# Split q and k in buffers per head, at two points of a pair's steps, and squares by ScalarE's Square

## The chip, the cores and the metric

One core of a Trainium2 chip runs the kernel. The metric is device time in microseconds (us) of one execution. The engines are named as in the profile: PE is TensorE (PEld its weight loads), DVE is VectorE, ACT is ScalarE, POOL is GpSimd, SP is the queue that issues all of this kernel's DMAs.

## The reference

Windowed attention with sink tokens feeds a two-layer network without a gate. `x` is the attention's output with the heads side by side, 3072 tokens by 512.

```python
# q, k, v: 4 batches x 8 heads x 768 positions x 64, float32; n_sink 4, window 128
scores = (1 / sqrt(64)) * q @ k.T
keep = (pos_k < n_sink) | ((pos_q - pos_k >= 0) & (pos_q - pos_k < window))
a = exp(where(keep, scores, -1e9) - max);  a = a / (sum(a) + 1e-9)
x = (a @ v)                                # w_in 512 x 2048, w_out 2048 x 512, float64
h = maximum(x @ w_in, 0);  out = (h * h) @ w_out
```

## The kernel before

The work is cut into 8 chunks of 384 tokens (`TOK`), half a sequence each, named `c`. The eight heads of a chunk go in four pairs, named `p`; `hh` is the head in the pair and `i` (0 to 2) the block of 128 queries. A tile's name in the program carries these numbers: `s_6_3_1_2` is the score of chunk 6, pair 3, head 1, block 2.

For precision a float32 number is carried as a rounded high part and the rest, both in the reduced format float32r. From pair 8 on (chunk 2) the scores are taken from such split tiles: `KS` holds high and low part of k, and `QS` the high part of q in 64 partitions and its low part in the other 64. `prep_q` makes `QS` with two casts on ACT (L215) and two subtractions on DVE (L217); `prep_k` makes `KS` with a cast on DVE (L223) and a subtraction on POOL (L224). There is one buffer of each (`ap1`), and one of the raw `qn` and `kn`.

A pair's steps are: six scores (L254 on PE; DVE's L258 adds the mask and takes the minimum into `nbs`; ACT's L261 takes the Exp and the sum), with a `normalise` on POOL behind the third and the sixth (L278, L283, and the sink columns into `PSK`, L289 and L292; DVE gives the reciprocal of the sums, L271 and L272). Then, while the next pair's scores run: transposes of head 0 and head 1 (`probs_of`, tile `pt`, copied out by DVE into `PTF`, L358 to L363), of the sinks' columns (`sink_keys`, tile `pss`), and the products with v (`values`, tile `xo`, L382). The scores, `pt` and `pss` share two PSUM banks in turn (tag `att`).

The network of an earlier chunk fills PE between these steps. For each of 16 slices of 128 hidden units there are 12 matmuls into `ph` (L454, weights `wi` in two parts against `x` in two parts), ACT's Relu into `r` (L462), the product `ph * r` on DVE (L466), its high part `gh` by a cast on ACT (L467), its low part `gl` on DVE (L471), and 9 matmuls into `po` for the slice before (L484, per token block two with `gh` and one with `gl`).

`slot(s)` lists the steps of pair `s`, mixed with the last steps of pair `s - 1`; the main loop deals these units out between the network's. Up to chunk 1 the order on each engine is that of the code (`manual_schedule`); from the first pair of chunk 2 on (`PAUSE`) a scheduler orders each engine's queue by the order of the code as priority and by its own costs. Every queue runs in order. `check_row` puts two more instructions on ACT now and then (L577, L579).

Of the kernel before, what the change touches and what calls it, by code (L numbers as in the profile page):

```python
# [40 lines left out]
def sink_window_attention_moe(  # L41
# [25 lines left out]
    with ExitStack() as fast:  # L67
# [143 lines left out]
        def prep_q(c, p):  # L211
            st = state[c, p]
            st["QS"] = QS = ap1.tile([P, 2, TOK], F32R, tag="QS", name=f"QS_{c}_{p}")
            for hh, own, oth in HALVES:
                nc.scalar.copy(QS[own, hh, :], st["qn"][own])  # L215
            for hh, own, oth in HALVES:
                nc.vector.tensor_tensor(QS[oth, hh, :], st["qn"][own], f32(QS[own, hh, :]), op=ALU.subtract)  # L217

        def prep_k(c, p):
            st = state[c, p]  # L220
            nk = st["nk"]
# [1 line left out]
            nc.vector.tensor_copy(KS[:, :, 0, 0:nk], st["kn"][:, :, 0:nk])  # L223
            nc.gpsimd.tensor_tensor(KS[:, :, 1, 0:nk], st["kn"][:, :, 0:nk], f32(KS[:, :, 0, 0:nk]), op=ALU.subtract)  # L224
# [5 lines left out]
        def score(c, p, hh, i, tag="att"):  # L230
# [16 lines left out]
            if c * NPAIR + p < NPS:  # L247
                own = HALVES[hh][1]
                KF = st["kn"][:, hh].rearrange("p n c -> p (n c)")
                nc.tensor.matmul(ps[:, 0:n], st["qn"][own, qcols], KF[own, c0 : c0 + n], start=True, stop=True)  # L250
            else:
                flat = st["KS"][:, hh].rearrange("p a n c -> p a (n c)")
                for a in range(2):
                    nc.tensor.matmul(  # L254
                        ps[:, 0:n], st["QS"][:, hh, qcols], flat[:, a, c0 : c0 + n], start=(a == 0), stop=(a == 1)
                    )
# [157 lines left out]

        def slot(s):

            nop = lambda: None
# [2 lines left out]
            pr = [nop] * 3  # L420
            if s + 1 < len(pairs) and s + 1 != PAUSE:
                n = pairs[s + 1]
                split = s + 1 >= NPS
                pr = [
                    lambda: split and prep_q(*n), lambda: split and prep_k(*n),
                    lambda: s + 2 != PAUSE and start_pair(s + 2),
                ]
            if s == PAUSE:
                units = sc + pr
            else:  # L430
                va = values_of(pairs[s - 1])
# [10 lines left out]
        def moe(legs):  # L442
# [3 lines left out]
            for n in range(len(items) + 1):  # L446
                if n < len(items):
# [18 lines left out]
                    nc.vector.tensor_tensor(ph[:, 0:TOK], ph[:, 0:TOK], r, op=ALU.mult)  # L466
                    nc.scalar.copy(gh, ph[:, 0:TOK])  # L467
# [484 lines left out]
```

## Time and profile before

| | |
|---|---|
| median of 3 runs | 737.74 us (737.46 to 737.82) |
| the profiled execution | 738.48 us, span of its instructions 736.6 us |
| busy share of the span | PE 95%, PEld 81%, DVE 68%, ACT 52%, POOL 30% |
| granted TensorE clock, mean | 0.991 |

A stretch in which PE is idle is lost to the whole, since PE's matmuls fill nearly all of the span; the other engines matter where PE waits for one of them. Matmuls overlap in the records, so a busy PE may still run below its pace.

### The profile page before, as it was taken

The page shows a single profiled execution, that of the slowest core. Times are in us where ns is not written, and L with a number is a line of the kernel's source. Part 1 is how long each engine was busy: PE and PEld are TensorE (multiplying, and loading weights), DVE is VectorE, ACT ScalarE, POOL GpSimd, SP SyncE. Part 2 cuts the span into 40 slices and gives each one's busy share as a digit, 9 for nine tenths or more (in the row PEclk, how much of TensorE's full clock was granted, in tenths as well). Part 3 has the DMA queues.
Part 4 walks back from the last instruction along what each step waited for, and adds up shares of the span by engine and source line. Part 5 has one row for each costly group of instructions (what it writes and reads, how often), then busy time and mean ns, then how long its engine had stood idle before and what let it go on. Part 6 is the DMA issues. An engine that isn't in the chain of part 4 may idle for free.

```text
span 736.6 us, 11643 instructions
## 1 busy us (share of the span) xinstructions
PE 698.4 (95%) x3866; PEld 599.6 (81%) x3866; DVE 502.4 (68%) x1254; ACT 381.2 (52%) x1074; POOL 223.6 (30%) x408
## 2 busy tenths in 40 slices
...
GB/s 233 154 177 186 130 140 191 176 91 60 133 60 81 156 91 70 97 129 91 100 99 77 133 112 88 96 114 113 95 60 112 85 55 16 1 1 44 0 1 47
DMA packets 37010, 71.75 MB, mean 97 GB/s; under 512 B 4368, under 2 KB 14096, under 8 KB 36944
## 3 DMA queue, kind: packets, MB, share of 16 engines
...
q8 instruction: 32, 0.52, 0.3%
...
## 4 chain that ended last, share of the span: by engine, by line
PE 63%; DVE 11%; ACT 3%; issue 3%; POOL 1%; DVEq 0%; POOLq 0%; ACTq 0%
PE po L484 26%; PE ph L454 25%; PE xo L382 4%; PE s L254 4%; DVE QS L217 3%; DVE rs L271 2%; PE pt L352 2%; DVE ph L466 1%; PE xo L385 1%; PE pss L299 1%; ACT P L261 1%; DVE gl L471 1%; ACT gh L467 1%; DVE KS L223 1%; DVE PTF L358 1%
## 5 line engine op out<-in xcount | busy, mean ns | idle before, releaser
L454 PE MATMUL ph<-x,wi 128*128 128x384 f32 x1536 | 309.9, 341 | 0.0
L454 PEld LDWEIGHTS ph<-x,wi 128*128 128x128 f32 x1536 | 265.4, 188 | 8.3 <-issue 1.7
L484 PE MATMUL po<-wo,gh 128*128 128x512 f32 x768 | 244.8, 399 | 4.9 <-ACT gh L467 4.9
L484 PEld LDWEIGHTS po<-wo,gh 128*128 128x128 f32 x768 | 136.7, 189 | 25.7 <-ACT gh L467 7.8
L484 PE MATMUL po<-wo,gl 128*128 128x512 f32 x384 | 152.8, 398 | 0.0
L261 ACT ACTIVATE P<-P,nbs 128x264 f32<-128x264 f32 (+1 forms) x192 | 94.7, 494 | 106.7 <-DVE nbs L258 95.6
L466 DVE TENSOR_TENSOR ph<-ph,r 128x384 f32<-128x384 f32 x128 | 71.9, 562 | 77.3 <-ACT r L462 76.7
L278 POOL TENSOR_TENSOR P<-P 128x256 f32<-128x256 f32 (+1 forms) x48 | 44.2, 921 | 246.8 <-ACT P L261 246.8
L467 ACT CAST gh<-ph 128x384 fp32r<-128x384 f32 x128 | 60.9, 476 | 98.6 <-DVE ph L466 97.5
L462 ACT ACTIVATE r<-ph 128x384 f32<-128x384 f32 x128 | 62.0, 484 | 90.2 <-PE ph L454 89.0
L283 POOL TENSOR_SCALAR P<-P,rs 128x136 f32<-128x136 f32 (+2 forms) x192 | 85.1, 460 | 61.7 <-DVE rs L272 30.3
L471 DVE TENSOR_TENSOR gl<-ph,gh 128x384 fp32r<-128x384 f32 x128 | 70.9, 554 | 42.6 <-ACT gh L467 41.6
L224 POOL TENSOR_TENSOR KS<-kn,KS 128x816 fp32r<-128x816 f32 (+1 forms) x24 | 59.2, 2465 | 102.2 <-DVE KS L223 67.2
L484 PEld LDWEIGHTS po<-wo,gl 128*128 128x128 f32 x384 | 72.2, 188 | 19.5 <-DVE gl L471 3.8
L258 DVE CUSTOM_DVE_ANT_0 P<-s,maskA 128x264 f32<-128x264 f32 x128 | 53.4, 426 | 40.2 <-PE s L254 38.4
L254 PE MATMUL s<-KS,QS 128*128 128x264 f32 (+1 forms) x288 | 58.7, 283 | 5.7 <-POOL KS L224 4.4
L254 PEld LDWEIGHTS s<-KS,QS 128*128 128x128 f32 x288 | 52.1, 188 | 13.8 <-POOL KS L224 5.4
L271 DVE TENSOR_SCALAR rs<-sm 128x3 f32<-128x3 f32 (+1 forms) x56 | 54.1, 967 | 8.3 <-ACT P L261 7.3
L382 PE MATMUL xo<-PTF,vn 128*64 128x256 f32 x448 | 48.3, 354 | 0.8 <-ACT PTF L341 0.7
L217 DVE TENSOR_TENSOR QS<-qn,QS 64x384 fp32r<-64x384 f32 x48 | 46.4, 966 | 2.2 <-ACT QS L215 0.8
L382 PEld LDWEIGHTS xo<-PTF,vn 128*64 128x64 f32 x448 | 32.3, 141 | 17.2 <-issue 6.3
L358 DVE TENSOR_TENSOR PTF<-pt,halves 128x256 f32<-128x256 f32 x96 | 36.2, 414 | 6.3 <-PE pt L352 6.0
...
## 6 DMA issues: line engine op xcount, KB each, us to landing
...
kn<-in_k_dram SPq DMA_DIRECT2D x24, 272.0 KB, 4.3
...
```

The lines of the kernel that those rows point to most:

```text
L217: nc.vector.tensor_tensor(QS[oth, hh, :], st["qn"][own], f32(QS[own, hh, :]), op=ALU.subtract)
L254: nc.tensor.matmul(ps[:, 0:n], st["QS"][:, hh, qcols], flat[:, a, c0 : c0 + n], start=(a == 0), stop=(a == 1))
L261: nc.scalar.activation(Pt[:, i, 0:n], Pt[:, i, 0:n], AF.Exp, bias=nb, scale=-1.0, accum_out=sm[:, i : i + 1])
L271: nc.vector.tensor_scalar(rs[:, hs], st["sm"][:, hs], EPS, None, op0=ALU.add)
L283: nc.gpsimd.tensor_scalar(Pt[:, j, 0:n], Pt[:, j, 0:n], rs[:, hh, j : j + 1], 1.0, op0=ALU.mult, op1=ALU.mult)
L382: nc.tensor.matmul(xo[h * D : h * D + D, cols], lhsT, rhs, start=(n == 0), stop=False, skip_group_check=True)
L454: nc.tensor.matmul(ph[:, 0:TOK], wi_at(i, cc, fc), xt[:, cc, :], start=(m == 0), stop=(m == 3 * NCC - 1),)
L462: nc.scalar.activation(r, ph[:, 0:TOK], AF.Relu)
L466: nc.vector.tensor_tensor(ph[:, 0:TOK], ph[:, 0:TOK], r, op=ALU.mult)
L467: nc.scalar.copy(gh, ph[:, 0:TOK])
L471: late = lambda: nc.vector.tensor_tensor(gl, ph[:, 0:TOK], f32(gh), op=ALU.subtract)
L484: nc.tensor.matmul(po[t], gt[:, ts_], wo[f][:, i, :], start=(f == f0 and j == 0), stop=(f == f1 - 1 and j == 2),)
```

## The change

`prep_q` and `prep_k` become `prep(s, hh)`, which makes one head's `KS` and `QS` in buffers of that head's own. In a pair's steps, `prep` of the next pair's head 0 stands behind the third score, that of head 1 behind the sixth, and the load of the next raw q and k (and this pair's v) opens the pair's steps. The transposes of head 1 now come ahead of the sinks'. In the network, `gh` is no longer a cast of the product but ACT's Square of `r`, issued right behind Relu; the product, for `gl`, stays on DVE.

```diff
-        def prep_q(c, p):
-            st["QS"] = QS = ap1.tile([P, 2, TOK], F32R, tag="QS", name=f"QS_{c}_{p}")
-            for hh, own, oth in HALVES:
-                nc.scalar.copy(QS[own, hh, :], st["qn"][own])
-            for hh, own, oth in HALVES:
-                nc.vector.tensor_tensor(QS[oth, hh, :], st["qn"][own], f32(QS[own, hh, :]), op=ALU.subtract)
-        def prep_k(c, p):
-            st["KS"] = KS = ap1.tile([P, 2, 2, 4, BS], F32R, tag="KS", name=f"KS_{c}_{p}")
-            nc.vector.tensor_copy(KS[:, :, 0, 0:nk], st["kn"][:, :, 0:nk])
-            nc.gpsimd.tensor_tensor(KS[:, :, 1, 0:nk], st["kn"][:, :, 0:nk], f32(KS[:, :, 0, 0:nk]), op=ALU.subtract)
+        def prep(s, hh):
+            _, own, oth = HALVES[hh]
+            KS = ap1.tile([P, 2, 4, BS], F32R, tag=f"KS{hh}", name=f"KS_{c}_{p}_{hh}")
+            QS = ap1.tile([P, TOK], F32R, tag=f"QS{hh}", name=f"QS_{c}_{p}_{hh}")
+            nc.vector.tensor_copy(KS[:, 0, 0:nk], st["kn"][:, hh, 0:nk])
+            nc.gpsimd.tensor_tensor(KS[:, 1, 0:nk], st["kn"][:, hh, 0:nk], f32(KS[:, 0, 0:nk]), op=ALU.subtract)
+            nc.scalar.copy(QS[own, :], st["qn"][own])
+            nc.vector.tensor_tensor(QS[oth, :], st["qn"][own], f32(QS[own, :]), op=ALU.subtract)
...
-                lambda: probs_of(*a, 0), lambda: sink_keys(*a), lambda: probs_of(*a, 1), lambda: values(*a),
+                lambda: probs_of(*a, 0), lambda: probs_of(*a, 1), lambda: sink_keys(*a), lambda: values(*a),
...
-                units = [
-                    sc[0], va[0], sc[1], va[1], sc[2], va[2], sc[3], va[3], sc[4], sc[5],
-                    pr[0], pr[1], pr[2],
-                ]
+            units = [
+                lambda: start_pair(s + 1), sc[0], va[0], sc[1], va[1], va[2], sc[2], lambda: prep(s + 1, 0),
+                va[3], sc[3], sc[4], sc[5], lambda: prep(s + 1, 1),
+            ]
...
                     nc.scalar.activation(r, ph[:, 0:TOK], AF.Relu)
-                    yield
                     gh = mp.tile([P, TOK], F32R, tag="gh", name=f"gh_{c}_{fc}")
                     gl = mp.tile([P, TOK], F32R, tag="gl", name=f"gl_{c}_{fc}")
+                    nc.scalar.activation(gh, r, AF.Square)
+                    yield
                     nc.vector.tensor_tensor(ph[:, 0:TOK], ph[:, 0:TOK], r, op=ALU.mult)
-                    nc.scalar.copy(gh, ph[:, 0:TOK])
```

The raw q and k of odd pairs in the first eight, which borrowed the `QS` and `KS` buffers, borrow those of head 0 now.

What this makes of the engines' queues is shown at one place, from the last score of pair (6,3) into pair (7,0). The line numbers of the changed kernel differ: L222 to L225 are `prep` (L223, L224, L215 and L217 before); the attention's are 1 higher (L259 is L258); in the network L441 is L454, L454 is L466, L458 is L471 and L471 is L484.

DVE before, from the mask of the last score on (rows that repeat are left out):

```order
L258 ISA P_6_3_1_6164,nbs_150<-s_6_3_1_2_6222,maskA_100 128x264
L223 CAST KS_7_0_6259<-kn_7_0_6036 128x2x544
L217 TENSOR_TENSOR QS_7_0_6244<-qn_7_0_6035,QS_7_0_6244 64x384
L271 TENSOR_SCALAR rs_6_3_1_6227<-sm_6_3_6049 128x3
L272 RECIPROCAL rs_6_3_1_6227<-rs_6_3_1_6227 128x3
L466 TENSOR_TENSOR ph_5_10_6215<-ph_5_10_6215,r_5_10_6242 128x384
L471 TENSOR_TENSOR gl_5_10_6250<-ph_5_10_6215,gh_5_10_6249 128x384
L258 ISA P_7_0_0_6286,nbs_150<-s_7_0_0_0_6287,maskA_100 128x264
```

DVE after, at the same place:

```order
L454 TENSOR_TENSOR ph_5_10_6290<-ph_5_10_6290,r_5_10_6309 128x384
L458 TENSOR_TENSOR gl_5_10_6312<-ph_5_10_6290,gh_5_10_6311 128x384
L259 ISA P_6_3_1_6297,nbs_150<-s_6_3_1_2_6326,maskA_100 128x264
L222 CAST KS_7_0_1_6349<-kn_7_0_6123 128x544
L225 TENSOR_TENSOR QS_7_0_1_6350<-qn_7_0_6122,QS_7_0_1_6350 64x384
L272 TENSOR_SCALAR rs_6_3_1_6331<-sm_6_3_6147 128x3
L273 RECIPROCAL rs_6_3_1_6331<-rs_6_3_1_6331 128x3
L454 TENSOR_TENSOR ph_5_11_6355<-ph_5_11_6355,r_5_11_6375 128x384
L458 TENSOR_TENSOR gl_5_11_6378<-ph_5_11_6355,gh_5_11_6377 128x384
L259 ISA P_7_0_0_6388,nbs_150<-s_7_0_0_0_6389,maskA_100 128x264
```

Half a cast and one subtraction stand between the last score and the reciprocal, where the whole cast and two subtractions stood, and the product and low part of slice 10 have moved ahead of that score.

POOL before, between the normalising of head 0 and of the next pair's head 0:

```order
L292 TENSOR_TENSOR PSK_142<-P_6_3_0_6050,PSK_142 128x2x8
L224 TENSOR_TENSOR KS_7_0_6259<-kn_7_0_6036,KS_7_0_6259 128x2x544
L278 TENSOR_TENSOR P_6_3_1_6164<-P_6_3_1_6164 128x2x128
L283 TENSOR_SCALAR P_6_3_1_6164<-P_6_3_1_6164,rs_6_3_1_6227 128x128
L283 TENSOR_SCALAR P_6_3_1_6164<-P_6_3_1_6164,rs_6_3_1_6227 128x136 x2
L289 CAST PSK_142<-P_6_3_1_6164 128x4x8
L278 TENSOR_TENSOR P_7_0_0_6286<-P_7_0_0_6286 128x3x128
```

POOL after:

```order
L293 TENSOR_TENSOR PSK_142<-P_6_3_0_6148,PSK_142 128x2x8
L223 TENSOR_TENSOR KS_7_0_1_6349<-kn_7_0_6123,KS_7_0_1_6349 128x544
L279 TENSOR_TENSOR P_6_3_1_6297<-P_6_3_1_6297 128x2x128
L284 TENSOR_SCALAR P_6_3_1_6297<-P_6_3_1_6297,rs_6_3_1_6331 128x128
L284 TENSOR_SCALAR P_6_3_1_6297<-P_6_3_1_6297,rs_6_3_1_6331 128x136 x2
L290 CAST PSK_142<-P_6_3_1_6297 128x4x8
L223 TENSOR_TENSOR KS_7_1_0_6495<-kn_7_1_6363,KS_7_1_0_6495 128x544
L279 TENSOR_TENSOR P_7_0_0_6388<-P_7_0_0_6388 128x3x128
```

A half of k stands ahead of the normalising of each head, where the whole stood ahead of head 1's.

PE before, from head 0's transposes on, in pair (7,0)'s first half (the rows of `ph` stand there twice, those of `po` three times or more):

```order
L352 MATMUL pt_6_3_0_6313<-ident_94,P_6_3_0_6050 128x128 x3
L484 MATMUL po_5_0_2_5722<-wo_10_1523,gh_5_10_6249 128x512 x2
L484 MATMUL po_5_0_2_5722<-wo_10_1523,gl_5_10_6250 128x512
L254 MATMUL s_7_0_0_1_6329<-KS_7_0_6259,QS_7_0_6244 128x264 x2
L454 MATMUL ph_5_12_6334<-x0_5_4741,wi_136 128x384 x2
L454 MATMUL ph_5_12_6334<-x1_5_4742,wi_136 128x384
L299 MATMUL pss_6_3_6341<-ident_94,PSK_142 128x128 x2
L254 MATMUL s_7_0_0_2_6353<-KS_7_0_6259,QS_7_0_6244 128x264 x2
L352 MATMUL pt_6_3_1_6386<-ident_94,P_6_3_1_6164 128x128 x3
```

PE after:

```order
L353 MATMUL pt_6_3_0_6406<-ident_94,P_6_3_0_6148 128x128 x3
L441 MATMUL ph_5_12_6413<-x0_5_4810,wi_136 128x384 x2
L441 MATMUL ph_5_12_6413<-x1_5_4811,wi_136 128x384
L255 MATMUL s_7_0_0_1_6420<-KS_7_0_0_6255,QS_7_0_0_6256 128x264 x2
L353 MATMUL pt_6_3_1_6436<-ident_94,P_6_3_1_6297 128x128 x3
L471 MATMUL po_5_0_0_5777<-wo_11_1565,gh_5_11_6377 128x512 x2
L471 MATMUL po_5_0_0_5777<-wo_11_1565,gl_5_11_6378 128x512
L300 MATMUL pss_6_3_6459<-ident_94,PSK_142 128x128 x2
L255 MATMUL s_7_0_0_2_6470<-KS_7_0_0_6255,QS_7_0_0_6256 128x264 x2
```

Head 1's transposes come 14 matmuls behind head 0's and ahead of the sinks', and the third score comes last.

More of the change, by code (lines that the diff above doesn't have):

```diff
@@ L209, in sink_window_attention_moe @@
         HALVES = ((0, lo_, hi_), (1, hi_, lo_))
-        def prep_q(c, p):
-            st = state[c, p]
-            st["QS"] = QS = ap1.tile([P, 2, TOK], F32R, tag="QS", name=f"QS_{c}_{p}")
-            for hh, own, oth in HALVES:
-                nc.scalar.copy(QS[own, hh, :], st["qn"][own])
-            for hh, own, oth in HALVES:
-                nc.vector.tensor_tensor(QS[oth, hh, :], st["qn"][own], f32(QS[own, hh, :]), op=ALU.subtract)
-        def prep_k(c, p):
+        def prep(s, hh):
+            if s >= len(pairs):
+                return
+            c, p = pairs[s]
             st = state[c, p]
             nk = st["nk"]
-            st["KS"] = KS = ap1.tile([P, 2, 2, 4, BS], F32R, tag="KS", name=f"KS_{c}_{p}")
-            nc.vector.tensor_copy(KS[:, :, 0, 0:nk], st["kn"][:, :, 0:nk])
-            nc.gpsimd.tensor_tensor(KS[:, :, 1, 0:nk], st["kn"][:, :, 0:nk], f32(KS[:, :, 0, 0:nk]), op=ALU.subtract)
+            _, own, oth = HALVES[hh]
+            KS = ap1.tile([P, 2, 4, BS], F32R, tag=f"KS{hh}", name=f"KS_{c}_{p}_{hh}")
+            QS = ap1.tile([P, TOK], F32R, tag=f"QS{hh}", name=f"QS_{c}_{p}_{hh}")
+            st["KS", hh], st["QS", hh] = KS, QS
+            nc.vector.tensor_copy(KS[:, 0, 0:nk], st["kn"][:, hh, 0:nk])
+            nc.gpsimd.tensor_tensor(KS[:, 1, 0:nk], st["kn"][:, hh, 0:nk], f32(KS[:, 0, 0:nk]), op=ALU.subtract)
+            nc.scalar.copy(QS[own, :], st["qn"][own])
+            nc.vector.tensor_tensor(QS[oth, :], st["qn"][own], f32(QS[own, :]), op=ALU.subtract)
         def bank(tag, name):
@@ L251, in score @@
             else:
-                flat = st["KS"][:, hh].rearrange("p a n c -> p a (n c)")
+                flat = st["KS", hh].rearrange("p a n c -> p a (n c)")
                 for a in range(2):
                     nc.tensor.matmul(
-                        ps[:, 0:n], st["QS"][:, hh, qcols], flat[:, a, c0 : c0 + n], start=(a == 0), stop=(a == 1)
+                        ps[:, 0:n], st["QS", hh][:, qcols], flat[:, a, c0 : c0 + n], start=(a == 0), stop=(a == 1)
                     )
```

22 lines of the change are left out of this document (4 added, 18 removed).

## The prediction

> **What bounds the kernel now.** I read the page's busy times and chain first, then the busy times by stage, then who TensorE (PE) waits for, then the timeline around one wait.
>
> ```profile
> PE 698.4 (95%) x3866; PEld 599.6 (81%) x3866; DVE 502.4 (68%) x1254; ACT 381.2 (52%) x1074; POOL 223.6 (30%) x408
> ...
> PE 63%; DVE 11%; ACT 3%; issue 3%; POOL 1%; DVEq 0%; POOLq 0%; ACTq 0%
> ```
>
> PE is busy 95% of the span and holds 63% of the chain that ended last. The change keeps every matmul, so it can only give back time in which PE stands still or runs slow: 736.6 - 698.4 = 38.2 us of idle PE. Where that lies (columns: the stretch, its length, busy time and instructions of PE, weight loads, DVE, ACT and POOL, granted clock, DMA):
>
> ```profile
> 0.00:99.00 99.00, 80.49 (x446) 59.35 (x447) 79.23 (x248) 67.11 (x177) 45.93 (x97) 0.97 0.55 172
> 99.00:153.00 54.00, 54.00 (x286) 48.77 (x285) 50.71 (x117) 33.96 (x69) 4.97 (x9) 1.00 0.53 171
> 153.00:231.50 78.50, 73.47 (x410) 63.33 (x409) 61.90 (x151) 33.57 (x91) 31.15 (x53) 0.98 0.27 76
> 231.50:317.50 86.00, 84.94 (x489) 74.64 (x489) 60.85 (x147) 50.44 (x157) 31.25 (x57) 1.00 0.38 111
> 317.50:406.00 88.50, 84.86 (x472) 72.53 (x471) 58.44 (x142) 49.79 (x157) 29.32 (x52) 1.00 0.35 98
> 406.00:490.50 84.50, 84.50 (x489) 74.48 (x489) 61.11 (x144) 50.33 (x157) 30.39 (x52) 1.00 0.36 106
> 490.50:579.00 88.50, 84.89 (x471) 72.52 (x470) 58.82 (x144) 49.81 (x157) 29.33 (x52) 1.00 0.35 97
> 579.00:665.00 86.00, 85.52 (x490) 75.12 (x489) 51.21 (x129) 30.05 (x78) 21.28 (x38) 1.00 0.09 25
> 665.00:736.60 71.60, 65.69 (x329) 58.86 (x327) 20.11 (x36) 16.11 (x33) 0.00 (x0) 0.98 0.07 24
> ```
>
> The start-up to 99 us holds 99 - 80.5 = 18.5 us of it, the end after 665 us 5.9 us. Scores there use unsplit q and k, or there are none, and only the squares change: I take nothing for both. In between PE idles 0, 5.03, 1.06, 3.64, 0, 3.61 and 0.48 us: 13.8 us. The stretches 317.5 to 406 and 406 to 490.5 each hold four pairs of heads; the second runs without a gap and is 4.0 us shorter. Who PE waits for from 140 us on (us in total, times, longest):
>
> ```profile
> PE po L484 <- ACT gh L467: 4.9, 5, 1.5
> PE s L254 <- POOL KS L224: 4.4, 4, 2.5
> PE pss L299 <- DVE PTF L361: 3.0, 7, 0.6
> PE s L254 <- DVE nbs L258: 1.4, 2, 0.9
> ```
>
> These four rows are 4.9 + 4.4 + 3.0 + 1.4 = 13.7 us, all but 0.1 of the idle time in the middle. Beside them weight loads (PEld) come late without PE going idle at once:
>
> ```profile
> PEld po L484 <- ACT gh L467: 7.8, 9, 1.8
> ...
> PEld po L484 <- DVE gl L471: 3.8, 13, 0.3
> ```
>
> One such place word for word: the end of pair (6,3), where the next pair's q and k are split (start, length, engine and line, in brackets the idle time before and its releaser):
>
> ```profile
> 545.59 0.41 PE L254 MATMUL s<-KS,QS 128*128 128x264 f32 x2
> ...
> 546.03 0.43 DVE L258 CUSTOM_DVE_ANT_0 P<-s,maskA 128x264 f32<-128x264 f32 x1 [1.56 <-PE s L254]
> 546.07 1.03 ACT L215 CAST QS<-qn 64x384 fp32r<-64x384 f32 x2
> ...
> 546.39 0.72 DVE L223 CAST KS<-kn 128x1088 fp32r<-128x1088 f32 x1
> ...
> 547.12 0.52 ACT L261 ACTIVATE P<-P,nbs 128x264 f32<-128x264 f32 x1
> 547.15 0.55 DVE L217 TENSOR_TENSOR QS<-qn,QS 64x384 fp32r<-64x384 f32 x1
> 547.25 2.85 POOL L224 TENSOR_TENSOR KS<-kn,KS 128x1088 fp32r<-128x1088 f32 x1 [7.25 <-DVE KS L223]
> ...
> 547.84 2.28 DVE L271 TENSOR_SCALAR rs<-sm 128x3 f32<-128x3 f32 x1
> ...
> 550.05 0.74 POOL L278 TENSOR_TENSOR P<-P 128x256 f32<-128x256 f32 x1
> 550.15 1.05 DVE L217 TENSOR_TENSOR QS<-qn,QS 64x384 fp32r<-64x384 f32 x1
> ...
> 551.23 0.18 DVE L272 RECIPROCAL rs<-rs 128x3 f32<-128x3 f32 x1
> ...
> 551.33 0.54 DVE L466 TENSOR_TENSOR ph<-ph,r 128x384 f32<-128x384 f32 x1
> 551.51 1.08 POOL L283 TENSOR_SCALAR P<-P,rs 128x128 f32<-128x128 f32 x3 [0.72 <-DVE rs L272]
> ...
> 551.90 0.48 ACT L467 CAST gh<-ph 128x384 fp32r<-128x384 f32 x1 [3.79 <-DVE ph L466]
> ...
> 552.41 0.56 DVE L471 TENSOR_TENSOR gl<-ph,gh 128x384 fp32r<-128x384 f32 x1 [0.55 <-ACT gh L467]
> ...
> 552.43 0.72 PE L484 MATMUL po<-wo,gh 128*128 128x512 f32 x2 [0.84 <-ACT gh L467]
> ```
>
> The last score ends near 546.0. From 547.25 to 550.10 POOL works out the low parts of k (L224). VectorE's (DVE) tiny L271 starts at 547.84 and takes 2.28 us, until POOL is through; the next L217 takes 1.05 us beside L278 instead of the 0.55 us of the one before. The squares (L466) come at 551.33, gh waits 3.79 us for them, and PE stands 0.84 us for gh.
>
> The Trainium skill, page "SBUF — State Buffer", section "Who interferes with whom", says that VectorE and GpSimd lock a shared port for a whole instruction and that the second to issue fully blocks. The rows above agree: 2.28 us for one DVE instruction and 1.05 us for another. By that rule the change also adds 24 lockings; the fourth rival says where that would bite.
>
> **The change part by part.**
>
> Splitting per head. Before, one KS and one QS buffer serve a pair, so the split can begin only behind the pair's sixth score, and the next pair's first score waits for it. Now head 0's halves are made behind the third score, about ten us ahead of their use, head 1's behind the sixth, with three scores, transposes and value matmuls between. The wait for KS (4.4 us) goes. Its longest, 2.5 us near 156 us, was followed by this:
>
> ```profile
> 156.20:160.20 4.00, 4.00 (x13) 3.58 (x14) 4.00 (x11) 2.62 (x6) 0.25 (x1) 0.57 0.62 168
> ```
>
> At a clock of 0.57, 4.0 us lose 4.0 x 0.43 = 1.7 us, and with the gap gone I count that as won too.
>
> The Trainium skill, page "TensorE: Matmul & The Clock Gate", Part 1, has the clock fall only after an idle window of about 3.4 us. PE's gap here was 2.5 us, so the trace differs, and the measurement decides. By that rule the drop would have another cause and could stay; the time would be 721.5 instead of 719.8 us.
>
> What the halves cost:
>
> ```profile
> L224 POOL TENSOR_TENSOR KS<-kn,KS 128x1088 fp32r<-128x1088 f32 x12 | 33.3, 2776 | 50.9 <-DVE KS L223 49.4 <-DVE rs L272 1.6
> ...
> L224 POOL TENSOR_TENSOR KS<-kn,KS 128x816 fp32r<-128x816 f32 x12 | 25.9, 2155 | 51.3 <-PE ph L454 32.1 <-DVE KS L223 17.8 <-DVE rs L272 1.3
> ```
>
> (2776 - 2155) / 272 elements = 2.28 ns per element and 294 ns fixed, so halves of 544 and 408 elements take 1.53 and 1.22 us: 24 x (1.53 + 1.22) = 66 us instead of 59.2, bounds 59 (halves exactly) and 118 (a half as dear as a whole). I take 66, since the two rows give the slope and hold lockings already. POOL is 30% busy. Each half stands ahead of its head's normalising, where the whole one stood ahead of head 1's alone: for head 0 up to 1.5 us, hidden by the half pair until its transposes, for head 1 see below. The k cast on DVE (0.72 us at 546.39) becomes two, together 0.72 to 1.44 us; I take 0.9, near the lower end, as L224's fixed part is small too. Even 0.72 more for each of four pairs adds 2.9 us to the 61.9 of 78.5 us of the densest stage, 153 to 231.5. The two q casts on ACT and two subtractions on DVE stay in number and move apart.
>
> The loads. `start_pair(s + 1)` now opens a pair's units where `start_pair(s + 2)` closed those of the pair before: the same point on SP's queue. New is that the first reader comes half a pair later, not a whole one. A pair takes 84.5 / 4 = 21 us, so about 10 us are left, less about 2 us until the last reader of the old k is through, for this landing:
>
> ```profile
> kn<-in_k_dram SPq DMA_DIRECT2D x24, 272.0 KB, 4.3
> ```
>
> 8 us against 4.3 us: hidden. If not, the split of head 0 slips, which still has some 8 us to its use.
>
> Square of r on ACT. The high part of the squares now follows Relu at once and waits for nothing.
>
> ```profile
> L471 DVE TENSOR_TENSOR gl<-ph,gh 128x384 fp32r<-128x384 f32 x128 | 70.9, 554 | 42.6 <-ACT gh L467 41.6 <-PE pt L352 0.5
> ...
> L467 ACT CAST gh<-ph 128x384 fp32r<-128x384 f32 x128 | 60.9, 476 | 98.6 <-DVE ph L466 97.5
> ...
> L577 ACT ACTIVATE sq<-half 128x256 bf16<-128x256 f32 x64 | 27.5, 429 | 0.5 <-DMA half<-in_moe_w_out_dram 0.4
> ```
>
> The cast at 476 ns is replaced by Square of the same shape; bounds 476 and 429 x 384 / 256 = 644 ns. I take 480, near the cast, the row of equal shape: nothing for ACT, 52% busy; at 644 it is 128 x 0.17 = 22 us on an engine with 355 us idle. DVE's low part gl no longer waits 0.55 us behind its own product for gh: 41.6 us of waiting go from the head of DVE's queue. gl itself still needs the product, so it is what could be late next.
>
> DVE's chain at the place above, reworked: L258 ends 546.47; half a cast 0.4; half L224 1.53, to 548.4, the subtraction of q (0.55) locked in beside it; ACT has one q cast less, so the Exp ends before that; L278 0.74 to 549.15 with L271 beside it; L272 0.18; product 0.54; gl 0.56: 550.4 instead of 552.97, 2.5 us earlier. PE wanted gh at 552.43 - 0.84 = 551.59 and gl two matmuls later, near 551.9. So the 4.9 us for gh go and no wait for gl replaces them. The wait of pss (3.0 us) is for DVE's copies of the transposes, which stand behind a gl that waits 0.55 us for gh, seven times 0.43 us on average; it goes too, as pss now stands behind pt of head 1 and more products. The two waits for nbs (1.4 us) I count as the same lateness of DVE.
>
> New order of transposes. Head 1's now come ahead of the sinks'. From the last score to them PE has 45 matmuls at (6,3); at 84.5 / 489 = 0.173 us each that is 7.8 us. POOL's normalising (L283) ended 552.59, 7.0 us behind the score's start, and by the sum above ends near 550.3, 4.7 us behind it. In 153 to 231.5 us, at pair (2,2), only 30 matmuls stand between, 5.2 us. If DVE is busy there some of three pairs wait: bounds 0 and 3 x (7.0 - 5.2) = 5.4 us; I take 1.0, as the chain there is shortened as well.
>
> The sum by stages: 153 to 231.5, 5.0 + 1.7 = 6.7; 231.5 to 317.5, 1.1; 317.5 to 406 between 3.6 (idle alone) and 88.5 - 472 x 0.173 = 6.9, I take 5.3, since a late load is partly hidden under the matmul ahead; 490.5 to 579 the same, 5.3; 579 to 665, 0.5. Together 18.9, less 1.0: 17.9 us. The profiled execution took 738.48 us (span 736.6 and 1.9 around it), so 720.6; the median of the runs, 737.74, is 0.7 below it: 719.8 us. With every upper bound, 1.7 + 1.7 + 1.0 more and nothing new: 715.4.
>
> **The rivals.**
> Second: the lock lasts as long as before and gl takes gh's place. For: gl hangs on the same DVE queue, and 13 late loads already wait for it. Against: L224's halves. At (6,3) gl would come right behind the product, 551.87 + 0.56 = 552.43, 0.5 us behind its need, so 0.5 / 0.84 of the 4.9 us stay (2.9), the 3.0 us of pss come back at pt, and the late loads (2 x 1.7) stay: 18.9 - 9.3 = 9.6 us won, 738.5 - 9.6 - 0.7 = 728.2 us.
> Third: no change, 736.3 to 739.2, the waits only passed on from pair to pair. Against: 406 to 490.5 shows that the same work runs without any.
> Fourth, slower: the transposes of head 1 wait for POOL in every pair, since half an L224 stands ahead of the normalising and the doubled lockings delay rs. Against: 7.8 us are left where 4.7 are needed. It begins above 7.8 us and decides from 7.8 + 18.9 / 24 = 8.6 us on; at 9 us it costs 24 x 1.2 = 28.8, 748 us.
>
> **How the numbers follow.** Likeliest, 0.70: 719.8, its own range 714 to 724. Second, 0.20: 728.2, between 724 and 732. Third 0.04, fourth 0.06. The range 714 to 730 takes in the first almost whole and most of the second. Runs of this kernel tell 0.2% from no change: faster by more than that 0.90, within it 0.04, slower 0.06.
>
> **What would show it.** Right: PE's waits for KS and for gh absent after 140 us, no clock below 1.00 near 156 us, L271 nowhere above about 1.1 us, the stretches that hold chunk 4's and chunk 6's pairs without idle PE, gh right behind r on ACT. Wrong: rows of PE waiting for gl, for transposes behind POOL's normalising, or for KS still; PE idle between 150 and 660 us above 6 us.

## The result, and the profile after

The changed kernel takes 719.72 us (median of 4 runs, 719.47 to 720.29), the one before 737.78 us on the same chip: a ratio of 0.9752, 95% interval 0.9735 to 0.9769. Forecast were 719.8 us. The profiled execution took 719.84 us, its span is 718.1 us.

The page's busy times and its chain, of the changed kernel:

```profile
PE 688.4 (96%) x3866; PEld 598.3 (83%) x3866; DVE 485.8 (68%) x1278; ACT 392.5 (55%) x1074; POOL 231.6 (32%) x432
...
PE 87%; DVE 6%; ACT 2%; POOL 2%; DMA 1%; issue 1%; SPq 0%; DVEq 0%; ACTq 0%; POOLq 0%
```

PE's idle time fell from 38.2 to 718.1 - 688.4 = 29.7 us, and its busy time, with the same 3866 matmuls, by 10.0 us. Both are won time: a matmul that waits for its weights or runs at a slow clock counts as busy. PE now holds 87% of the chain. The stages, cut at the first scores of pairs and besides at 155.5 and 645 us (columns as before):

```profile
0.00:98.50 98.50, 78.65 (x446) 58.28 (x446) 78.38 (x249) 67.43 (x176) 45.08 (x98) 0.97 0.56 173
98.50:155.50 57.00, 56.81 (x298) 51.10 (x297) 53.42 (x121) 35.25 (x69) 5.71 (x7) 1.00 0.51 164
155.50:226.50 71.00, 68.72 (x399) 59.52 (x398) 55.08 (x155) 34.10 (x93) 32.87 (x60) 1.00 0.31 85
226.50:310.60 84.10, 84.10 (x489) 74.43 (x488) 58.79 (x150) 51.29 (x156) 33.35 (x61) 1.00 0.38 109
310.60:393.20 82.60, 82.60 (x471) 73.11 (x470) 55.03 (x146) 52.08 (x157) 30.33 (x56) 1.00 0.37 105
393.20:477.30 84.10, 84.10 (x489) 74.56 (x488) 58.10 (x148) 52.20 (x157) 31.98 (x56) 1.00 0.37 107
477.30:559.80 82.50, 82.50 (x469) 73.00 (x469) 55.69 (x150) 52.07 (x157) 30.33 (x56) 1.00 0.37 105
559.80:645.00 85.20, 85.20 (x491) 75.18 (x490) 51.07 (x128) 31.43 (x79) 21.93 (x40) 1.00 0.09 27
645.00:718.10 73.10, 65.74 (x329) 59.13 (x328) 20.24 (x36) 16.63 (x33) 0.00 (x0) 0.98 0.07 23
```

From 226.5 to 645 us PE has no gap at all. Who it waits for from 140 us on (us in total, times, longest), all three rows of it:

```profile
PE s L255 <- DVE nbs L259: 1.0, 1, 1.0
PE pt L353 <- DVE PTF L362: 0.7, 1, 0.7
PE po L471 <- DVE ob L490: 0.4, 1, 0.4
```

2.1 us where 13.7 stood; KS, gh and pss are gone from the list, and no row for gl has come. The place that the prediction went through, the end of pair (6,3):

```profile
533.03 0.41 PE L255 MATMUL s<-KS,QS 128*128 128x264 f32 x2
...
533.47 0.43 DVE L259 CUSTOM_DVE_ANT_0 P<-s,maskA 128x264 f32<-128x264 f32 x1
...
533.83 0.44 DVE L222 CAST KS<-kn 128x544 fp32r<-128x544 f32 x1
...
534.30 0.55 DVE L225 TENSOR_TENSOR QS<-qn,QS 64x384 fp32r<-64x384 f32 x1
534.41 1.66 POOL L223 TENSOR_TENSOR KS<-kn,KS 128x544 fp32r<-128x544 f32 x1 [4.90 <-DVE KS L222]
...
534.89 1.21 DVE L272 TENSOR_SCALAR rs<-sm 128x3 f32<-128x3 f32 x1
...
536.13 0.18 DVE L273 RECIPROCAL rs<-rs 128x3 f32<-128x3 f32 x1
536.28 0.49 ACT L449 ACTIVATE r<-ph 128x384 f32<-128x384 f32 x1 [0.62 <-PE ph L441]
...
536.81 0.53 ACT L452 ACTIVATE gh<-r 128x384 fp32r<-128x384 f32 x1
536.81 0.57 DVE L454 TENSOR_TENSOR ph<-ph,r 128x384 f32<-128x384 f32 x1 [0.50 <-ACT r L449]
...
537.51 0.56 DVE L458 TENSOR_TENSOR gl<-ph,gh 128x384 fp32r<-128x384 f32 x1
```

From the start of the last score to the end of the reciprocal it is 3.3 us now and was 5.8. DVE's tiny L272 is still held by POOL, for 1.21 instead of 2.28 us, and afterwards DVE waits 0.50 us for r, where it used to be behind. Square (L452) starts right behind Relu, beside the product. The groups that the change touched (busy time and mean ns of one, idle time ahead):

```profile
L458 DVE TENSOR_TENSOR gl<-ph,gh 128x384 fp32r<-128x384 f32 x128 | 71.0, 555 | 10.2 <-DVE ph L454 0.5
L452 ACT ACTIVATE gh<-r 128x384 fp32r<-128x384 f32 x128 | 67.2, 525 | 3.5
...
L223 POOL TENSOR_TENSOR KS<-kn,KS 128x544 fp32r<-128x544 f32 x24 | 39.2, 1632 | 137.8 <-DVE KS L222 130.9 <-PE ph L441 6.8
...
L223 POOL TENSOR_TENSOR KS<-kn,KS 128x408 fp32r<-128x408 f32 x24 | 32.2, 1342 | 188.4 <-DVE KS L222 185.1 <-PE ph L441 3.3
```

### The profile page after: what moved, and what is told of

It reads as the page before. It is cut to its first block, busy times and chain, and to the rows that moved or that the text cites. A ratio compares the mean times of both kernels' runs of the same rounds, so it can differ in the third digit from the quotient of the medians.

```text
span 718.1 us, 11750 instructions
## 1 busy us (share of the span) xinstructions
PE 688.4 (96%) x3866; PEld 598.3 (83%) x3866; DVE 485.8 (68%) x1278; ACT 392.5 (55%) x1074; POOL 231.6 (32%) x432
## 4 chain that ended last, share of the span: by engine, by line
PE 87%; DVE 6%; ACT 2%; POOL 2%; DMA 1%; issue 1%; SPq 0%; DVEq 0%; ACTq 0%; POOLq 0%
PE ph L441 35%; PE po L471 35%; PE xo L383 5%; PE s L255 4%; PE pt L353 2%; PE xo L386 1%; PE s L251 1%; PE pt L335 1%; DVE P L259 1%; PE pss L300 1%; POOL P L284 1%; DMA kn<-in_k_dram 1%; ACT P L262 1%; DVE t L535 0%; DVE ph L454 0%
## 5 line engine op out<-in xcount | busy, mean ns | idle before, releaser
L441 PE MATMUL ph<-x,wi 128*128 128x384 f32 x1536 | 306.7, 340 | 0.0
L441 PEld LDWEIGHTS ph<-x,wi 128*128 128x128 f32 x1536 | 264.9, 188 | 8.2 <-issue 1.7
L471 PE MATMUL po<-wo,gh 128*128 128x512 f32 x768 | 244.0, 398 | 0.4 <-DVE ob L490 0.4
L223 POOL TENSOR_TENSOR KS<-kn,KS 128x408 fp32r<-128x408 f32 (+1 forms) x48 | 71.4, 1487 | 326.2 <-DVE KS L222 316.1
L471 PE MATMUL po<-wo,gl 128*128 128x512 f32 x384 | 151.4, 394 | 0.0
L471 PEld LDWEIGHTS po<-wo,gh 128*128 128x128 f32 x768 | 135.8, 188 | 18.7 <-issue 0.7
L454 DVE TENSOR_TENSOR ph<-ph,r 128x384 f32<-128x384 f32 x128 | 71.7, 560 | 64.7 <-ACT r L449 63.9
L284 POOL TENSOR_SCALAR P<-P,rs 128x136 f32<-128x136 f32 (+2 forms) x192 | 82.3, 447 | 43.1 <-DVE rs L273 25.5
L471 PEld LDWEIGHTS po<-wo,gl 128*128 128x128 f32 x384 | 72.0, 188 | 16.1
L259 DVE CUSTOM_DVE_ANT_0 P<-s,maskA 128x264 f32<-128x264 f32 x128 | 53.8, 429 | 46.2 <-PE s L255 43.7
L458 DVE TENSOR_TENSOR gl<-ph,gh 128x384 fp32r<-128x384 f32 x128 | 71.0, 555 | 10.2 <-DVE ph L454 0.5
L452 ACT ACTIVATE gh<-r 128x384 fp32r<-128x384 f32 x128 | 67.2, 525 | 3.5
L255 PE MATMUL s<-KS,QS 128*128 128x264 f32 (+1 forms) x288 | 57.2, 281 | 1.2 <-DVE nbs L259 1.0
L272 DVE TENSOR_SCALAR rs<-sm 128x3 f32<-128x3 f32 (+1 forms) x56 | 47.3, 844 | 3.1 <-ACT P L262 2.0
L279 POOL TENSOR_TENSOR P<-P 128x256 f32<-128x256 f32 (+1 forms) x48 | 43.4, 903 | 16.7 <-ACT P L262 16.7
L383 PE MATMUL xo<-PTF,vn 128*64 128x256 f32 x448 | 46.5, 345 | 0.9 <-ACT PTF L342 0.9
L383 PEld LDWEIGHTS xo<-PTF,vn 128*64 128x64 f32 x448 | 31.6, 138 | 18.1 <-issue 9.9
L394 ACT CAST x<-xo 128x384 fp32r<-128x384 f32 x32 | 15.3, 480 | 54.0 <-PE xo L386 53.9
```

Of the source, the lines that this page charges most:

```text
L223: nc.gpsimd.tensor_tensor(KS[:, 1, 0:nk], st["kn"][:, hh, 0:nk], f32(KS[:, 0, 0:nk]), op=ALU.subtract)
L255: nc.tensor.matmul(ps[:, 0:n], st["QS", hh][:, qcols], flat[:, a, c0 : c0 + n], start=(a == 0), stop=(a == 1))
L259: nc.vector.tensor_tensor_reduce(Pt[:, i, 0:n], ps[:, 0:n], mask[:, 0:n], -SCALE, BIG, ALU.add, ALU.min, nb)
L284: nc.gpsimd.tensor_scalar(Pt[:, j, 0:n], Pt[:, j, 0:n], rs[:, hh, j : j + 1], 1.0, op0=ALU.mult, op1=ALU.mult)
L383: nc.tensor.matmul(xo[h * D : h * D + D, cols], lhsT, rhs, start=(n == 0), stop=False, skip_group_check=True)
L441: nc.tensor.matmul(ph[:, 0:TOK], wi_at(i, cc, fc), xt[:, cc, :], start=(m == 0), stop=(m == 3 * NCC - 1),)
```

## The experiments

Each kernel is compared with the kernel before on its own chip (three chips, 739.7 to 740.1 us), and the changed kernel was run again on one of them. The table has each stage's length in us in the profiled execution, from the first score of a pair to that of the next one named, worked out from start times rounded to 0.1 us, so a length can be 0.1 us off; the last column is PE's idle time in the whole span.

| kernel | start to (2,0) | to (3,1) | to (4,1) | to (5,1) | to (6,1) | to (7,1) | to the end | PE idle |
|---|---|---|---|---|---|---|---|---|
| before | 99.0 | 132.5 | 86.0 | 88.3 | 84.7 | 88.3 | 157.8 | 38.2 |
| after | 98.5 | 128.0 | 84.1 | 82.6 | 84.1 | 82.5 | 158.3 | 29.7 |
| after, again | 100.4 | 127.5 | 84.2 | 82.5 | 84.2 | 82.5 | 158.3 | 28.8 |
| Square alone | 100.2 | 132.8 | 85.7 | 85.0 | 84.2 | 85.1 | 164.7 | 40.8 |
| Square alone, k first | 98.5 | 130.9 | 85.1 | 85.1 | 84.1 | 85.2 | 157.6 | 35.1 |
| k first alone | 100.0 | 132.0 | 85.8 | 88.1 | 84.7 | 88.1 | 157.6 | 38.5 |
| split alone | 100.2 | 128.5 | 84.8 | 82.5 | 84.7 | 82.6 | 159.1 | 29.6 |
| old order | 100.0 | 126.8 | 84.3 | 82.4 | 84.2 | 82.5 | 157.0 | 26.3 |
| swapped buffers | 102.0 | 126.5 | 84.7 | 82.4 | 84.2 | 82.4 | 157.1 | 24.8 |
| both of these | 100.9 | 126.0 | 85.1 | 82.3 | 84.3 | 82.3 | 157.4 | 26.7 |
| both, sinks' split earlier | 97.8 | 126.2 | 85.1 | 82.3 | 84.3 | 82.4 | 157.5 | 25.2 |
| one buffer | 99.6 | 130.5 | 87.5 | 82.4 | 85.0 | 82.4 | 157.4 | 31.6 |
| subtraction twice | 100.8 | 127.7 | 85.2 | 82.6 | 84.1 | 82.6 | 158.7 | 29.6 |
| subtraction four times | 105.2 | 142.9 | 91.6 | 82.5 | 88.7 | 82.5 | 164.6 | 52.7 |

**Square alone, in the kernel before.**

```diff
                     nc.scalar.activation(r, ph[:, 0:TOK], AF.Relu)
-                    yield
...
+                    nc.scalar.activation(gh, r, AF.Square)
+                    yield
                     nc.vector.tensor_tensor(ph[:, 0:TOK], ph[:, 0:TOK], r, op=ALU.mult)
-                    nc.scalar.copy(gh, ph[:, 0:TOK])
```

> Square alone in the kernel before: q and k are split for the whole pair as before, with one buffer. Theory A (the prediction's: the end of a pair was late by the long lock AND by gh's way over the product): the waits for KS, the slow clock behind the longest and the two for nbs stay (4.4 + 1.7 + 1.4 us); gl takes gh's place at the pair's end, so 2.9 of the 4.9 us for gh stay; the 3.0 us for pss go. About 5 us won: 732.8 us (731 to 735). Theory B (gh's way over the product was all; the lock harms nothing once gh is early): 4.9 + 3.0 + 3.4 us of late loads go: 726.5 us (725 to 728). Theory C (a wait that is taken away turns up one pair later): 736 us or more.

738.66 us, ratio 0.9990 (0.9974 to 1.0006): no change, the number of theory C, though for another reason. PE's two largest waits from 140 us on:

```profile
PE s L254 <- POOL KS L224: 9.5, 6, 2.8
PE po L484 <- DVE gl L471: 3.4, 4, 1.2
```

The waits for gh and pss are gone, and (4,1) to (5,1) and (6,1) to (7,1) are 3.2 to 3.3 us shorter each, with gl in gh's place, as theory A said. But the end grew by 6.9 us: the KS waits doubled. At pairs (7,2) and (7,3) POOL's subtraction (L224) stands in its queue behind the normalising of head 1 (L283) here, and ahead of it in the kernel before: the scheduler re-sorted it. And a long wait can cost twice, by the idle time and by a slow clock behind it (columns as in the stages, the clock third from the end), here in the 4 us behind waits of 2.79, 1.91 and 2.52 us, the first and the third of which were followed by a clock of 0.57 and 0.60:

```profile
158.20:162.20 4.00, 4.00 (x14) 3.49 (x13) 3.74 (x10) 2.81 (x7) 0.00 (x0) 0.57 0.60 170
...
595.50:599.50 4.00, 4.00 (x24) 3.70 (x24) 1.78 (x6) 1.62 (x4) 0.00 (x0) 1.00 0.56 139
622.60:626.60 4.00, 3.98 (x15) 3.66 (x16) 0.47 (x3) 0.61 (x2) 0.00 (x0) 0.60 0.00 0
```

**The split alone: the changed kernel with Square undone** (gh a cast of the product again; from 142 us on PE's order is the changed kernel's but for four matmuls near 214 us).

> The changed kernel with the Square undone: gh is again the cast of the product, the buffers per head and the new order stay. Theory A: the waits for KS and nbs and the slow clock go (7.5 us), and with DVE's chain 2.5 us earlier at the pair's end the 4.9 us for gh and the 3.4 us of late loads go as well; some of the 3.0 us for pss stay, since gl waits 0.55 us for gh again: 722 us (720 to 724). Theory B: only the 7.5 us go and PE's waits for gh stay at 4 to 5 us: 730.3 us (728 to 732).

723.70 us, ratio 0.9793 (0.9769 to 0.9816): theory A. The whole list of PE's waits from 140 us on, and the row of weight loads for gl:

```profile
PE s L255 <- DVE nbs L259: 1.1, 2, 0.6
PE pt L353 <- DVE PTF L362: 1.1, 2, 0.9
PE po L471 <- DVE ob L490: 0.4, 1, 0.4
```

```profile
PEld po L471 <- DVE gl L458: 2.6, 8, 0.5
```

No wait for gh although gh still hangs on the product: at the pair's end it was DVE that was late, not gh's way. No wait for pss either, although some of it was expected to stay. Against 0.9727 to 0.9752 for the changed kernel (two chips), Square adds 3 to 5 us to this: the late loads for gl, and 0.5 to 1.0 us in four of the stages.

**Square alone, with k split ahead of q.** The first run left open whether Square is worth nothing by itself or was robbed by that re-sorting. Writing the split of k first brings POOL's subtraction back ahead of the normalising at both pairs.

```diff
-                    lambda: split and prep_q(*n), lambda: split and prep_k(*n),
+                    lambda: split and prep_k(*n), lambda: split and prep_q(*n),
```

> Square alone in the kernel before, as in the first run, but with the pair's k split ahead of its q (cast and subtraction of k written first). In the first run POOL's subtraction for pairs (7,2) and (7,3) had slipped behind the normalising of head 1, and PE waited there 2.2 and 3.0 us for KS with a slow clock behind; here it stands ahead of that again. Theory L (Square has a gain of its own, which that order ate): KS waits fall from 9.5 to about 4.4 us and the slow clock after 620 us (0.83 over 10 us) goes: 738.7 - 5.1 - 1.7 = 731.9 us (730 to 734). Theory M (Square alone is worth nothing while one buffer keeps the split at the pair's end): 737 to 740 us.

729.87 us, ratio 0.9874 (0.9853 to 0.9895): theory L, just below its range. The control, without Square:

> The control to that: the kernel before with k split ahead of q and nothing else, gh still the cast of the product. Under theory L the KS waits shrink by 0.5 to 1 us each (4.4 us in four places) and the 4.9 us for gh stay: 735 to 738 us, 3 us or more above the run with Square. Under theory M: equal to it.

738.11 us, 0.9976 (0.9962 to 0.9990), 0.1 us above the range of theory L. So Square by itself is worth 738.11 - 729.87 = 8.2 us once the order is right. That it was the order that hid this in the first run is shown: of the 3866 matmuls, PE works all but two at the same place of its order in both runs with Square, and the stretch to the end is 157.6 instead of 164.7 us. PE's largest waits from 140 us on, first with Square, then of the control:

```profile
PE po L484 <- DVE gl L471: 4.8, 5, 1.4
PE pss L299 <- DVE PTF L361: 1.7, 2, 1.6
PE s L254 <- POOL KS L224: 0.9, 1, 0.9
```

```profile
PE po L484 <- ACT gh L467: 5.7, 6, 1.5
PE pss L299 <- DVE PTF L361: 4.0, 7, 1.6
PE s L254 <- DVE QS L217: 1.5, 1, 1.5
...
PE s L254 <- POOL KS L224: 0.9, 1, 0.9
```

With the split still at the pair's end gl does take gh's place. The wait for KS is 0.9 us in the control too, 3.5 us less than before, yet only about 2 us of the time are won: a wait of 1.5 us for QS has come, and those for gh and pss are 0.8 and 1.0 us longer. The two parts overlap: alone they win 8.2 us and 2.1% of 739.7, 15 us, together about 18 to 20.

**The old order of transposes in the changed kernel.**

```diff
-                lambda: probs_of(*a, 0), lambda: probs_of(*a, 1), lambda: sink_keys(*a), lambda: values(*a),
+                lambda: probs_of(*a, 0), lambda: sink_keys(*a), lambda: probs_of(*a, 1), lambda: values(*a),
```

> The changed kernel with the sinks' transposes back ahead of head 1's. Theory A (pss waited because DVE's copies stood behind a gl that waited for gh): the order is worth nothing now, 719.2 to 720.7 us, PE's waits for pss below 0.5 us from 140 us on. Theory D (the new order itself took the 3.0 us away): 722 to 723.5 us with PE's waits for pss near 3 us. If head 1's transposes were kept waiting by POOL in the dense stage, this order would win up to 1 us there: 718.7 us.

718.24 us, 0.9719 (0.9695 to 0.9744), PE's waits for pss 0.7 us in one place, where theory A named less than 0.5: nearest to theory A, 1 us below its range. Theory D falls: without the new order the 3.0 us do not come back. Against 0.9752 and 0.9727 for the changed kernel the intervals overlap, so whether the new order costs the 1.0 us that was forecast stays open.

**Swapped buffers: head 0's half behind the sixth score again.** Writing both halves at the pair's end would not be enough, as the scheduler is free to put head 0's earlier once its buffer is free; so the buffers are swapped from pair to pair as well.

```diff
-            KS = ap1.tile([P, 2, 4, BS], F32R, tag=f"KS{hh}", name=f"KS_{c}_{p}_{hh}")
-            QS = ap1.tile([P, TOK], F32R, tag=f"QS{hh}", name=f"QS_{c}_{p}_{hh}")
+            KS = ap1.tile([P, 2, 4, BS], F32R, tag=f"KS{(hh + s) % 2}", name=f"KS_{c}_{p}_{hh}")
+            QS = ap1.tile([P, TOK], F32R, tag=f"QS{(hh + s) % 2}", name=f"QS_{c}_{p}_{hh}")
...
-                lambda: start_pair(s + 1), sc[0], va[0], sc[1], va[1], va[2], sc[2], lambda: prep(s + 1, 0),
-                va[3], sc[3], sc[4], sc[5], lambda: prep(s + 1, 1),
+                lambda: start_pair(s + 1), sc[0], va[0], sc[1], va[1], va[2], sc[2],
+                va[3], sc[3], sc[4], sc[5], lambda: prep(s + 1, 0), lambda: prep(s + 1, 1),
```

> The changed kernel, but head 0 of a pair takes the buffers that head 1 of the pair before held, and both halves are written at the pair's end: so head 0's half can be made only behind the sixth score, as all of it was before, and head 1's is the early one. Theory A by the sum's numbers: from the last score to the next pair's first PE has some 27 matmuls of 0.173 us, 4.7 us, and the half is through 0.43 + 0.44 + 1.63, about 3 us behind the score; so the wait for KS stays away except in the dense stage, where it was 2.5 us with the whole (0.72 + 2.85 us) and is about 1 us with the half: 719.7 to 722 us. Theory E (head 0's early place is what removes the wait): the KS waits and the slow clock come back, 4.4 + 1.7 us: 726 us.

718.81 us, 0.9726 (0.9702 to 0.9751), with no wait for KS from 140 us on: just below theory A's range. Theory E falls; that it is head 0's half that is early is worth nothing (head 1's is the early one here).

**One buffer for both heads, halves kept.** `KS` and `QS` are tiles of the pair again, and both halves are made at its end, as in the swap's last four lines.

```diff
-            KS = ap1.tile([P, 2, 4, BS], F32R, tag=f"KS{hh}", name=f"KS_{c}_{p}_{hh}")
-            QS = ap1.tile([P, TOK], F32R, tag=f"QS{hh}", name=f"QS_{c}_{p}_{hh}")
+            if hh == 0:
+                st["KSp"] = ap1.tile([P, 2, 2, 4, BS], F32R, tag="KS0", name=f"KS_{c}_{p}")
+                st["QSp"] = ap1.tile([P, 2, TOK], F32R, tag="QS0", name=f"QS_{c}_{p}")
+            KS, QS = st["KSp"][:, hh], st["QSp"][:, hh]
```

> The changed kernel, but both heads' split tiles lie in one buffer per pair as before, so both halves must wait for the sixth score; cast, subtraction and q stay halved per head, and Square and the order of transposes stay. Theory F (what pays is that half of the work leaves the pair's end, for which the second buffer is needed): gl or gh and KS are late at the pair's end again, PE idles 8 us or more in them, 728 to 736 us. Theory G (what pays is that one instruction holds DVE up for 1.2 instead of 2.3 us, and that the first score waits for its own half alone): 719 to 722 us.

727.46 us, 0.9833 (0.9805 to 0.9861), 7.1 us above the changed kernel on the same chip, just short of theory F's range, and for the most part with other waits than it named (gl has 0.5 us). The two largest:

```profile
PE s L257 <- DVE nbs L261: 4.2, 3, 2.2
PE pt L355 <- DVE PTF L364: 1.2, 1, 1.2
```

PE waits for DVE to empty a score's bank. The longest of these, at 233.4 us, is made here (lines are 2 higher; L225 is POOL's subtraction, L224 and L227 the k cast and the q subtraction on DVE):

```profile
227.09 1.68 POOL L225 TENSOR_TENSOR KS<-kn,KS 128x544 fp32r<-128x544 f32 x1 [1.48 <-DVE KS L224]
...
227.57 1.50 DVE L224 CAST KS<-kn 128x544 fp32r<-128x544 f32 x1
...
228.99 0.97 DVE L274 TENSOR_SCALAR rs<-sm 128x3 f32<-128x3 f32 x1
...
229.90 1.35 POOL L225 TENSOR_TENSOR KS<-kn,KS 128x544 fp32r<-128x544 f32 x1
...
230.00 1.67 DVE L227 TENSOR_TENSOR QS<-qn,QS 64x384 fp32r<-64x384 f32 x1
```

None of these instructions takes longer than 1.7 us, yet three of DVE in a row take 4.1 us. What counts here is how much of POOL's work meets DVE's at the pair's end, not the longest single hold. The swapped buffers are the closest comparison: the same order of writing, PE's order the same but for 26 of 3866 matmuls, and half of the work gone from the pair's end: a ratio of 0.9726 instead of 0.9833. But it is chunks 2 and 3 that pay (130.5 and 87.5 against 126.5 and 84.7 us) and, by 0.8 us, chunk 5. In the stages of chunks 4 and 6 one buffer is as good (82.4 us): what the change wins there needs no second buffer.

**POOL's subtraction done twice, and four times.** For four times the line is repeated three times.

```diff
             nc.gpsimd.tensor_tensor(KS[:, 1, 0:nk], st["kn"][:, hh, 0:nk], f32(KS[:, 0, 0:nk]), op=ALU.subtract)
+            nc.gpsimd.tensor_tensor(KS[:, 1, 0:nk], st["kn"][:, hh, 0:nk], f32(KS[:, 0, 0:nk]), op=ALU.subtract)
```

> The changed kernel with each of POOL's subtractions for the low part of k done twice, so POOL is 1.63 or 1.34 us later at each head. Theory H (POOL has slack: in the trace head 1's transposes start 2.8 us or more behind the normalising in 18 of 24 pairs, 0.6 to 1.3 us in the others, most of them in chunks 2 and 3): 719.8 to 723 us. Theory I (the rival of the prediction: every us that POOL holds DVE up comes back as idle PE): 24 x 2.97 = 71 us of it, half of that beside other work: 740 us or more.

723.23 us, 0.9771 (0.9741 to 0.9801), 2.9 us above the changed kernel on the same chip: theory H, 0.2 us above its range. POOL is 59.6 us busier, DVE 0.9 us. Theory I falls for a reason in these rows, DVE beside a repeated subtraction (lines are 1 higher; L224 is the repeat, L455 the product):

```profile
539.85 1.38 POOL L224 TENSOR_TENSOR KS<-kn,KS 128x544 fp32r<-128x544 f32 x1
...
539.93 0.57 DVE L455 TENSOR_TENSOR ph<-ph,r 128x384 f32<-128x384 f32 x1 [0.50 <-ACT r L450]
...
540.63 0.56 DVE L459 TENSOR_TENSOR gl<-ph,gh 128x384 fp32r<-128x384 f32 x1
...
541.11 0.42 DVE L260 CUSTOM_DVE_ANT_0 P<-s,maskA 128x264 f32<-128x264 f32 x1
```

Product, gl and mask, which read PSUM, keep their 0.57, 0.56 and 0.42 us.

> The changed kernel with each of POOL's subtractions for the low part of k done four times. Repeated, one takes 1.39 or 1.13 us, so POOL is 4.2 or 3.4 us later at each head. Theory H (POOL is hidden until head 1's normalising ends later than PE comes to its transposes, 8 us behind the last score in most pairs, 5.3 us in chunk 2): the normalising that ended 4.8 us behind the score now ends at 9.0, about 1 us late in some 15 pairs and 2.4 us in three: 20 to 25 us, 740 to 748 us, in rows of PE waiting for POOL's normalising. If POOL's time stays hidden, 723 to 730 us.

757.54 us, 1.0245 (1.0217 to 1.0273), 37 us above the changed kernel (run on another chip) where 20 to 25 were expected. The idle time is as expected, 52.7 - 28.8 = 23.9 us; the rest is busy time of PE, 705.3 instead of 690.8 us, part of it at a clock of 0.59 to 0.72 in the 4 us behind four gaps. The place was wrong for the most part: PE waits 2.5 us for the normalising, 5.8 us for the sinks' columns that POOL writes behind it, and 8.3 us for DVE's copies of the network's output (`ob`); DVE waits 27.3 us for loads of k, which were hidden in the changed kernel (1.4 us). A likely reason, not tested, is that POOL reads their buffer longer now.

**Both variants together, and one in the start-up.** As the old order and the swap both came out under the changed kernel, it was run again beside a kernel with the two edits together.

> The changed kernel again, on the chip of the next three, to set them beside it: 719.7 us (718.5 to 721), 2.2 to 2.7% under the kernel before.

> The changed kernel with the sinks' transposes back ahead of head 1's and with head 0 taking the buffers that head 1 of the pair before held. Theory J (the 126.8 and 126.5 us from chunk 2's first pair to chunk 3's second in those two runs, against 128.0, were theirs, and add up in part): 716.5 to 718.5 us, 0.2 to 0.4% under the changed kernel of this call. Theory K (the difference was the chip's): the same as the changed kernel of this call within 0.15%.

720.34 us (719.97 to 721.43), 0.9727 (0.9699 to 0.9755), and 718.99 us (717.34 to 720.03), 0.9703 (0.9675 to 0.9732), on one chip: 0.19% less, between theory K (within 0.15%) and theory J (0.2 to 0.4%), with runs that just touch. From (2,0) to (3,1) it is 126.0 instead of 127.5 us, and PE's only wait after 140 us is 0.3 us for nbs. It has the lowest ratio of the study, by a margin at the edge of what can be told; the intervals of the old order and of the swap overlap with it.

The start-up's edit, on top of both:

```diff
             for s in range(NPAIR + 1):
+                if s == 2:
+                    split_sinks()
                 for i, tags in enumerate((("att", "att"), ("h", "h"), ("o0", "o1"))):
...
-                if s == 2:
-                    split_sinks()
```

> The run with old order and swapped buffers, and in the start-up the split of the sinks' values (VS) written ahead of the third pair's scores instead of behind them: in the changed kernel PE waits 2.0 us for it near 26 us. If that wait is on the path: 1 to 2 us less, 717 to 718 us, 0.9685 of the kernel before. If DVE, 80% busy in the start-up, is late with the masks instead: no change, 718.5 to 719.5 us.

719.03 us, 0.9723 (0.9705 to 0.9741): no change, although PE's wait for VS (1.7 us in the run without this edit) is gone from the profile.

## Why the prediction was right, step by step

**The sum.** Forecast were 17.9 us, the span fell by 18.5. By stages (forecast, measured): start 0 and 0.5; (2,0) to (3,1), 6.7 less 1.0 and 4.5; to (4,1), 1.1 and 1.9; to (5,1), 5.3 and 5.7; to (6,1), 0 and 0.6; to (7,1), 5.3 and 5.8; the rest 0.5 and -0.5. The total is closer than the terms, and that is luck: 1.2 us too much in the dense stage and 1.0 too much in the rest stand against 0.4 to 0.8 too little in each of the five others. In the rest, PE ends its work 1.0 us sooner, but from its last matmul to the end of the span it is 7.4 us where it was 5.9 (6.0 to 8.1 in the other runs), a part that the sum did not have. The middle of idle time alone and full pace (3.6 and 6.9) was the right choice for the two stages that carry most.

**KS.** The wait went, and with it the slow clock (1.00 from 154 to 170 us). The Trainium skill's rule on the page "TensorE: Matmul & The Clock Gate", Part 1, would have left the drop; the measurement decided for the gap, and in the run with Square alone both came back (2.79 us, 0.57). But the reason was wrong in part: "made about ten us ahead of their use" is not needed, as the swapped buffers show. For this wait the second buffer is not needed either: with one buffer KS is not among PE's waits. What the prediction does not name is that `prep` also writes k ahead of q; that alone, in the control, takes the wait for KS from 4.4 to 0.9 us, though 1.5 us for QS come instead. The second buffer pays through DVE instead: without it the lateness of the pair's end turns up as waits for nbs (4.2 us).

**gh and the hold by POOL.** The chain to the reciprocal was worked out as ending at 549.15 + 0.18 = 549.33, 3.7 us behind the score's start; it is 3.3 us, since L272 (L271 before) ended with POOL's subtraction and was not held by the row behind it on POOL (L279, L278 before), as the sum had it. The rest of the chain does not stand as forecast: it had the product of slice 10 behind the reciprocal, and in the changed queue this product and its gl stand ahead of the last mask; behind the reciprocal comes slice 11's. So that no wait for gl came has two possible reasons, the shorter hold and the new place of the product. Every run with the new list of units has both, and the two stages that gain most are 82.3 to 82.6 us in all of them, with one buffer or two and with Square or without; the runs with the old list and the whole split have 85.0 us at best. Which of the halves and the new list does it there was not tested. That gh's wait at the pair's end goes without Square is shown by the split alone.

**Rival two** described the mechanism rightly and its condition too: gl takes gh's place where the whole split stays at the pair's end in one piece (3.4 and 4.8 us), and not where half of it has left.

**pss.** Two reasons were given, that gl no longer waits for gh and that pss stands behind more products, and either is enough beside the split: with the old order and Square 0.7 us are left, with the new order and without Square none (head 1's transposes then wait 1.1 us for PTF). The 1.0 us for head 1's transposes was the wrong kind: the 2.1 us of waits left are for nbs, PTF and ob.

**Sizes.** Square took 525 ns, forecast 480 between 476 and 644, hidden as said. POOL's halves took 1.63 and 1.34 us, forecast 1.53 and 1.22; repeated, when no instruction of DVE is in the way at the start, 1.39 and 1.13. The two k casts of 439 ns are the 0.9 us taken. L272's longest is 1.23 us, just above the "about 1.1" that was named as a sign of being right. PE idles 2.3 us between 150 and 660, under the 6 set as the limit.

**Rival four** is real but far: twice the work costs 2.9 us, four times 37, most of it not in the place that the rival named.
